# Batch 0 of a fused attention-and-MoE kernel: states first in the load queue, x in four pair loads, attention head pair by head pair, the first S·W as S·W1 − S·W2, and a column of ones for the state-read sums

## The chip, the cores and the metric

The kernel runs on one core of a Trainium2 chip. The metric is the device time of one execution in microseconds (us); of several runs the median is given. An execution is also taken by the hardware profiler; its trace is what the rows below show. The engines are TensorE (PE for matmuls, PEld for loads of its stationary operand), VectorE (DVE), ScalarE (ACT), GpSimd (POOL) and SyncE (SP, which here only issues DMAs). Each engine works off its own list of instructions in the order in which they are written.

## The reference, cut to what matters

```python
B, H, S, Ns, D = 8, 8, 512, 32, 64            # x: B,H,S,D   state: B,H,Ns,D   float32
a     = softmax(scale * x @ state.T)           # over the 32 states
xread = a @ state                              # S rows per batch
a2    = softmax(scale * state @ x.T)           # over the 512 tokens
sread = a2 @ x                                 # Ns rows per batch
t = concat([xread, sread], axis=2)             # then tokens x (H*D = 512), 4352 of them
out = maximum(t @ w1, t @ w2) @ w_out          # d_ff = 1024
```

## The kernel before

maximum(h1, h2) is computed as relu(h1 − h2) + h2. So a batch needs t @ (w1 − w2), its relu times w_out, and t @ (w2 w_out). The kernel builds `wd` = w1 − w2 and `wwo` = w2 w_out on the chip, in bf16. For the S rows of a batch t is a @ state, so the kernel multiplies the states into the weights once per batch: `sw` makes SW = state · [wd | wwo], 1024 + 512 columns, in two halves g of four heads each, with the states laid out in block-diagonal pairs of heads in `sbd` (four pairs k of two heads). `l1` then multiplies the transposed attention weights `AT` by SW and applies relu into `R`; `l2` adds R · w_out (`l2_f`) and AT · SW's last 512 columns (`l2_open`) into one PSUM bank per token block c of 128 tokens (NC = 4), copies it out and stores it. `sread_mm` computes the state reads, the unnormalised e.T @ x, and with eight more matmuls of one column each the sums of e that `sread_norm` divides by; `sread_tr` transposes them, and `moe_sread` sends all batches' state reads through the MoE at the end.

The weights come in four quarters q of 256 columns of d_ff: `load_wq` brings w2, w1 and w_out of a quarter (512 KB each), `w2_cast` and `wo_cast` make bf16, `w_sub` subtracts, `w2_tr` transposes w2, `w_wo` adds up w2 w_out. Batch 0 is worked off quarter by quarter as the weights land, with its four l2 sums open in `ACC` for the whole time (that takes the four banks of the PSUM pool `pa`); batch 1's attention (`states` for batches 1 to 7, `cast_x`, `xt_pe`, `scores`, `norm`, `at_pe`) is put between its quarters. This part, up to batch 1's first l1, is called the ramp below. After it a loop runs over the batches 1 to 7: eight l1 blocks, the scores of the next batch, four l2 blocks with `sw` of the next batch between them. Batches 2 to 7 get x transposed by DMA instead of by TensorE.

The schedule is written by hand: every engine, and SP's queue of loads, follows the order of the calls in the code (`engs` and `eng` arguments choose V, A or P for a copy). SP issues a DMA only when its buffer is free and when an earlier DMA has landed (eight at a time are under way). `idle(n)` issues n matmuls on zeros. A pool's buffer comes free when its last reader is done.

Of the kernel before, what the change touches and what calls it, by code (L numbers as in the profile page):

```python
# [15 lines left out]
def kernel(  # L16
# [59 lines left out]
    sfr = stage.tile([112, 2, 512], F32, name="sfr")  # L76
    sbr = stage.tile([112, 8, 2, D], BF16, name="sbr")
    sread_t = consts.tile([128, 4, B * Ns], BF16, name="sread_t")
# [3 lines left out]

    def load_x(b):
        xf = xio.tile([128, H, NC * D], F32, tag="xf", name="xf")
        xf_t[b] = xf
        for g in range(2):
            nc.sync.dma_start(
                out=xf[:, 4 * g:4 * g + 4, :],
                in_=x[b, 4 * g:4 * g + 4].rearrange("h (p c) d -> p h (c d)", c=NC),
            )  # L90
# [9 lines left out]

    def load_states(t, lo, hi):
        s = state[lo:hi].rearrange("b (k j) (l m) d -> (b k) l j (m d)", j=2, l=4)
        if hi - lo == 1:
            for j in range(2):
                nc.scalar.dma_start(out=t[:, j, :], in_=s[:, :, j, :])
        else:
            for j in range(2):
                nc.sync.dma_start(out=t[:, j, :], in_=s[:, :, j, :])


    def states(sf, sb, lo, hi, ceng, e0, e1, pool=None):
        nb = hi - lo
        copy(ceng, sb.rearrange("p m j d -> p j m d"), sf.rearrange("p j (m d) -> p j m d", m=8))
        p = bank(BF16, pool)
        n = nb * 16
        for m in range(8):
            nc.tensor.transpose(p[:, m * n:(m + 1) * n], sb[:, m].rearrange("p j d -> p (j d)"), ident[0:n, 0:n])
        for j, e in ((0, e0), (1, e1)):
            o = sbd[64 * j:64 * j + 64, lo:hi, :, 32 * j:32 * j + 32].rearrange("p b k (l m) -> p (b k) l m", l=4)
            i = p[64 * j:64 * j + 64, 0:8 * n].rearrange("p (m k l) -> p k l m", m=8, l=4)  # L120
            copy(e, o, i)


# [26 lines left out]
    def scores(b, hh, pool=None):  # L150
        d = st[b]
        if hh == 0:
            d["e"] = at.tile([128, 2, NC, 4, Ns], BF16, tag="e", name="e")
            d["a"] = at.tile([128, 2, NC, 4, Ns], BF16, tag="a", name="a")
            d["es"] = at.tile([128, 2, 2 * NC, 2], F32, tag="es", name="es")
            d["er"] = at.tile([128, 2, 2 * NC, 2], F32, tag="er", name="er")
# [38 lines left out]
    def sread_mm(b, pool=None):  # L195
        d = st[b]
        p = bank(F32, pool)
        d["srp"] = p
        for c in range(NC):
            xv = d["xb"][:, c].rearrange("p (i g d) -> p g i d", g=2, d=D)  # L200
            for g in range(2):
                for ih in range(2):
                    nc.tensor.matmul(p[64 * ih:64 * ih + 64, g * 128:(g + 1) * 128],  # L203
                                     d["e"][:, g, c, 2 * ih:2 * ih + 2].rearrange("p i n -> p (i n)"),
                                     xv[:, g, 2 * ih:2 * ih + 2],
                                     start=(c == 0 and g == 0), stop=(c == NC - 1 and g == 1), skip_group_check=True)
        for g in range(2):
            for c in range(NC):
                nc.tensor.matmul(p[:, 256 + g:257 + g], d["e"][:, g, c].rearrange("p i n -> p (i n)"), ones[:, 0:1],  # L209
                                 start=False, stop=(c == NC - 1), skip_group_check=True)  # L210

    def sread_norm(b):
# [4 lines left out]
        d["sr"] = sr  # L217
        nc.vector.reciprocal(rr, p[:, 256:258])
        for g in range(2):
            nc.vector.tensor_scalar(sr[:, :, g, :], p[:, g * 128:(g + 1) * 128].rearrange("p (i d) -> p i d", i=2),  # L220
                                    scalar1=rr[:, g:g + 1], scalar2=None, op0=ALU.mult)

# [10 lines left out]
    def sw(b, lo, hi, engs=("V", "A"), pool=None):  # L233
# [9 lines left out]
        for g in range(2):  # L243
            copy(engs[g], SW[b][:, g, lo:hi], pg[g][:, 0:n])

    flip = [0]
# [45 lines left out]
    def moe_sread():  # L292
        NT = B * Ns
        r = big.tile([128, NF, NT], BF16, tag="rs", bufs=1, name="rs")
        for f in range(NF):
# [4 lines left out]
            relu(r[:, f, :], p[:, 0:NT])  # L300
        ob = big.tile([128, NT // 128, DM], F32, tag="obs", bufs=1, name="obs")
        for t in range(NT // 128):
# [30 lines left out]

    def w_wo(half, i):
        p = bank()
        for j in range(4):
            f = 4 * half + j
            nc.tensor.matmul(p, w2t[:, f, i, :], wo[:, f, :], start=(j == 0), stop=(j == 3))  # L338
        if half == 0:
            copy("A" if i % 2 else "V", w2acc[:, i, :], p)  # L340
        else:
            nc.vector.tensor_tensor(wwo[:, i, :], p, w2acc[:, i, :], op=ALU.add)

    def idle(n):
        p = bank(F32, pa)
        for j in range(n):
            nc.tensor.matmul(p, wz[:, 0:128], wz, start=True, stop=True)

# [5 lines left out]


    load_states(sf0, 0, 1)
    load_x(0)
    for q in range(3):
        load_wq(q)
    load_states(sfr, 1, B)  # L360
    load_x(1)
# [9 lines left out]


    idle(7)
    states(sf0, sb0, 0, 1, "V", "A", "V", pa)
    cast_x(0, ("V", "V"))
    xt_pe(0, 0, "A", pa)
    xt_pe(0, 1, "V", pa)
    w2_cast(0, "P")
    scores(0, 0)
    w2_tr(0, "A")  # L380
    norm(0, 0, "V")
    scores(0, 1)
# [69 lines left out]
    for b in range(1, B):  # L452
# [61 lines left out]
```

## Time and profile before

| | us |
|---|---|
| median of 3 runs | 171.64 (171.13 to 173.83) |
| the profiled execution, its own time | 172.71 |
| its span, first to last instruction | 170.9 |
| PE busy in the span | 147.9 (87%) |
| DVE, ACT, POOL busy | 89.7, 66.6, 38.0 |

The profiled execution's own time stands 0.6% over the median of the runs. The span is 1.8 us shorter than its own time. Busy shares are averages over a ramp in which PE waits and a loop in which it does not, so they are to be read stretch by stretch.

### The profile page before, as it was taken

Reading aid. Unit: us, or ns where it says so; the run is one execution under the profiler, and the core shown is the slowest. Engines: PE = TensorE matmul, PEld = TensorE weight load, DVE = VectorE, ACT = ScalarE, POOL = GpSimd, SP = SyncE. Lnnn points to the kernel's source line nnn. Section 1 sums busy time; section 2 is a strip of 40 time slices with the busy share of each in tenths; the row PEclk is TensorE's granted clock in tenths of the full one; section 3 lists DMA queues with packets and bytes.
Section 4 is the critical chain, followed back from the end, with each engine's and each line's share of the span. In section 5 each row is a group of like instructions: output and inputs, shape, how many; then the busy total and the mean of one; then the engine's idle time right before and its main releaser. Section 6 shows DMA issues by size and latency. Waiting matters only on the chain.

```text
span 170.9 us, 2878 instructions
## 1 busy us (share of the span) xinstructions
PE 147.9 (87%) x1164; PEld 73.7 (43%) x1183; DVE 89.7 (52%) x163; ACT 66.6 (39%) x127; POOL 38.0 (22%) x41
## 2 busy tenths in 40 slices
PE   7053769959498999999999999999999999999990
PEld 2043534545253344453444445444444544574440
DVE  2158663663667692475458248645815854551110
ACT  3024424365414753382255237316424631730111
POOL 1055361200850031404043040403400040000000
PEclk9999999987999999999999999999999999999999
DMA  5999999910060497598948559685830620501333
GB/s 172 318 373 359 292 324 356 339 47 4 2 119 4 180 125 184 192 271 117 288 157 217 125 183 296 110 266 186 194 61 2 247 52 10 244 6 39 85 123 123
DMA packets 34561, 29.02 MB, mean 170 GB/s; under 512 B 19572, under 2 KB 31860, under 8 KB 33652
## 3 DMA queue, kind: packets, MB, share of 16 engines
q1 hardware_dynamic: 34508, 28.77, 59.3%
q8 instruction: 9, 0.15, 0.3%
q10 hardware_dynamic: 40, 0.07, 0.1%
q14 instruction: 4, 0.03, 0.1%
HBM read 15.20 MB, written 8.91 MB: 141 GB/s over the span
## 4 chain that ended last, share of the span: by engine, by line
PE 80%; DVE 8%; ACT 4%; DMA 3%; issue 2%; ACTq 1%; DVEq 0%
PE acc L274 33%; PE ps L264 16%; PE acc L270 9%; PE ps L241 4%; PE ps L338 4%; DMA sf<-in_state_dram 3%; PE ps L203 2%; PE ps L298 2%; PE ps L162 2%; PE acc L308 2%; DVE xb L60 2%; DVE wd L328 1%; PE ps L209 1%; DVE es L172 1%; PE acc L306 1%
## 5 line engine op out<-in xcount | busy, mean ns | idle before, releaser
L274 PE MATMUL acc<-wo,r 128*128 128x512 bf16 x252 | 60.7, 383 | 0.4 <-ACT xt L58 0.2
L274 PEld LDWEIGHTS <-r 128*128 128x128 bf16 x256 | 25.1, 99 | 30.1 <-issue 1.3
L264 PE MATMUL ps<-aT,sw 128*128 128x512 bf16 x127 | 30.2, 385 | 3.2 <-DVE sw L60 2.8
L255 DVE TENSOR_SCALAR r<-ps 128x512 bf16<-128x512 f32 x32 | 22.1, 692 | 19.6 <-PE ps L264 19.6
L58 ACT CAST sw<-ps 128x512 bf16<-128x512 f32 (+1 forms) x26 | 14.3, 555 | 33.3 <-PE ps L241 23.0
L174 POOL TENSOR_TENSOR a<-e,er 128x512 bf16<-128x512 bf16 x14 | 14.4, 1049 | 56.7 <-DVE er L173 42.6
L253 ACT ACTIVATE r<-ps 128x512 bf16<-128x512 f32 x32 | 19.3, 604 | 9.0 <-PE ps L264 7.7
L60 DVE CAST sw<-ps 128x512 bf16<-128x512 f32 (+1 forms) x26 | 16.5, 643 | 11.1 <-PE ps L241 11.0
L60 DVE COPY ob<-acc 128x512 f32<-128x512 f32 x16 | 10.8, 672 | 21.8 <-PE acc L274 21.6
L58 ACT COPY ob<-acc 128x512 f32<-128x512 f32 x16 | 9.4, 585 | 27.7 <-PE acc L274 26.8
L264 PEld LDWEIGHTS <-sw 128*128 128x128 bf16 x128 | 12.1, 99 | 16.5 <-DVE sw L60 3.1
L62 POOL CAST xb<-xf 128x1024 bf16<-128x1024 f32 x12 | 12.3, 1039 | 23.4 <-DMA xf<-in_x_dram 23.4
L270 PE MATMUL acc<-sw,aT 128*128 128x512 bf16 x52 | 16.2, 381 | 1.0 <-DVE sw L60 0.2
L172 DVE TENSOR_REDUCE es<-e 128x16 f32<-128x512 bf16 x16 | 10.6, 661 | 4.0 <-ACT e L165 3.9
L165 ACT ACTIVATE e<-ps 128x512 bf16<-128x512 f32 x16 | 8.8, 595 | 3.4 <-PE ps L162 2.6
L241 PE MATMUL ps<-wd,sbd 64*32 64x512 bf16 (+1 forms) x144 | 7.2, 369 | 2.2 <-DVE wd L328 1.7
L241 PEld LDWEIGHTS <-sbd 64*32 64x32 bf16 x208 | 3.3, 89 | 11.6 <-issue 11.3
L328 POOL TENSOR_TENSOR wd<-w1f,w2f 128x512 bf16<-128x512 f32 x4 | 5.1, 1267 | 9.6 <-DMA w1f<-in_moe_w_dram 9.6
L338 PE MATMUL ps<-wo,w2t 128*128 128x512 bf16 x31 | 7.0, 379 | 0.1
L270 PEld LDWEIGHTS <-aT 128*128 128x128 bf16 x64 | 4.4, 97 | 4.8 <-issue 3.1
L162 PEld LDWEIGHTS <-xt 128*128 128x128 bf16 x128 | 5.4, 103 | 1.7
L162 PE MATMUL ps<-sbd,xt 128*128 128x64 bf16 x128 | 5.7, 200 | 0.0
(78 smaller groups left out, 119.0 us busy)
## 6 DMA issues: line engine op xcount, KB each, us to landing
xf<-in_x_dram SPq DMA_DIRECT2D x16, 512.0 KB, 4.9
out_dram<-ob SPq DMA_DIRECT2D x7, 1024.0 KB, 5.7
w2f<-in_moe_w_dram SPq DMA_DIRECT2D x4, 512.0 KB, 9.9
w1f<-in_moe_w_dram SPq DMA_DIRECT2D x4, 512.0 KB, 11.1
wof<-in_moe_w_out_dram SPq DMA_DIRECT2D x4, 512.0 KB, 10.6
out_dram<-ob SPq DMA_DIRECT2D x2, 512.0 KB, 2.6
out_dram<-obs SPq DMA_DIRECT2D x8, 64.0 KB, 1.7
sfr<-in_state_dram SPq DMA_DIRECT2D x2, 224.0 KB
```

The lines of the kernel that those rows point to most:

```text
L58: nc.scalar.copy(o, i)
L60: nc.vector.tensor_copy(o, i)
L162: nc.tensor.matmul(pv[:, c, kk], d["xt"][:, c, k, :], sbd[:, b, k, :], start=(c == 0 and kk == 0), stop=(c == NC - 1 and kk == 1))
L172: nc.vector.tensor_reduce(d["es"][:, hh], ev, axis=mybir.AxisListType.X, op=ALU.add)
L174: (nc.gpsimd if eng == "P" else nc.vector).tensor_mul(av, ev, d["er"][:, hh].unsqueeze(3).to_broadcast([128, 2 * NC, 2, Ns]))
L241: nc.tensor.matmul(pg[g][32 * i:32 * i + 32, 0:n], sbd[64 * g:64 * g + 64, b, i, 32 * g:32 * g + 32], rhs, start=True, stop=True)
L253: nc.scalar.activation(out=o, in_=p, func=ACTF.Relu)
L255: nc.vector.tensor_scalar(o, p, scalar1=0.0, scalar2=None, op0=ALU.max)
L264: nc.tensor.matmul(p, SW[b][:, g, f * 128:(f + 1) * 128], AT[b][:, g].rearrange("p c t -> p (c t)"), start=(g == 0), stop=(g == 1))
L270: nc.tensor.matmul(p, AT[b][:, g, c, :], SW[b][:, g, FF:WC], start=(start and g == 0), stop=(stop and g == 1))
L274: nc.tensor.matmul(p, R[b][:, f, c * 128:(c + 1) * 128], wo[:, f, :], start=(start and j == 0), stop=(stop and j == len(fs) - 1))
L338: nc.tensor.matmul(p, w2t[:, f, i, :], wo[:, f, :], start=(j == 0), stop=(j == 3))
```

## The change

Five things are done. First, the states of batch 0 are loaded by one DMA at the head of SP's queue into 128 partitions (before: two DMAs on ACT's queue into 16 partitions); one transpose then gives `sbd` of batch 0 where eight did, and a negated copy `sbdn` is made. Second, x of batch 0 is loaded in four DMAs of one head pair each, and cast (POOL), transposed, scored and normalised pair by pair. Third, the first 256 columns of SW are computed as sbd · w1 + sbdn · w2 from bf16 copies of w1 and w2 (`sw_first`), so that they do not wait for wd. Fourth, for batches 2 to 7 a copy of x in bf16 with a 65th column of ones per head (`xo`) feeds `sread_mm`, and the eight matmuls of one column go; `cast_x1` makes the copy on POOL. Fifth, the order of the ramp is rewritten: `w_sub` goes to one engine per quarter (POOL, V, V, V), `w_wo` is done in three parts of 2, 4 and 2 blocks, fillers (`idle`) stand between the steps of the head, and in the loop all three parts of `sw` stand together behind the second l2.

```diff
-    sf0 = stage.tile([16, 2, 512], F32, name="sf0")
-    sb0 = stage.tile([16, 8, 2, D], BF16, name="sb0")
+    sf0 = stage.tile([128, 2 * D], F32, name="sf0")
+    sb0 = stage.tile([128, 2 * D], BF16, name="sb0")
+    sbdn = stage.tile([128, 4, 2 * Ns], BF16, name="sbdn")
+    w1b = stage.tile([128, 4, FQ], BF16, name="w1b")
...
+    def load_state0():
+        nc.sync.dma_start(out=sf0.rearrange("p (j d) -> p j d", j=2),
+                          in_=state[0].rearrange("(k j) n d -> n k j d", j=2))
+
+    def state0():
+        nc.vector.tensor_copy(sb0, sf0)
+        p = bank(BF16, pa)
+        nc.tensor.transpose(p[:, 0:128], sb0, ident)
+        for j, e in ((0, "A"), (1, "V")):
+            copy(e, sbd[64 * j:64 * j + 64, 0, :, 32 * j:32 * j + 32],
+                 p[64 * j:64 * j + 64, 0:128].rearrange("p (n k) -> p k n", k=4))
+        nc.vector.tensor_scalar(sbdn, sbd[:, 0], scalar1=-1.0, scalar2=None, op0=ALU.mult)
...
+    def cast_x1(b):
+        xo = stage.tile([128, NC, H, 66], BF16, tag="w1f", bufs=3, name="xo")
+        nc.gpsimd.memset(xo[:, :, :, 64:65], 1.0)
+        for g in range(2):
+            nc.gpsimd.tensor_copy(xo[:, :, 4 * g:4 * g + 4, 0:D].rearrange("p c i d -> p i c d"),
+                                  xf_t[b][:, 4 * g:4 * g + 4, :].rearrange("p i (c d) -> p i c d", c=NC))
...
+    def sw_first(engs):
+        SW[0] = big.tile([128, 2, WC], BF16, tag="sw", name="sw")
+        pg = [bank(), bank()]
+        for t, w in ((sbd[:, 0], w1b), (sbdn, w2b[0])):
+            for i in range(4):
+                for g in range(2):
+                    nc.tensor.matmul(pg[g][32 * i:32 * i + 32, 0:FQ], t[64 * g:64 * g + 64, i, 32 * g:32 * g + 32],
+                                     w[64 * g:64 * g + 64, i, :], start=(w is w1b), stop=(w is not w1b))
+        for g in range(2):
+            copy(engs[g], SW[0][:, g, 0:FQ], pg[g][:, 0:FQ])
...
-    load_states(sf0, 0, 1)
-    load_x(0)
+    load_state0()
+    load_x(0, 4)
...
+    idle(3)
+    state0()
+    idle(2)
+    for k in range(4):
+        cast_pair(0, k, "P")
+    xt_pair(0, 0, "A")
...
+    norm_pair(0, 0, "P")
     w2_cast(0, "P")
+    scores_pair(0, 2)
+    idle(2)
+    norm_pair(0, 1, "P")
+    scores_pair(0, 3)
+    copy("P", w1b.rearrange("p i f -> p (i f)"), w1f[0].rearrange("p i f -> p (i f)"))
+    norm_pair(0, 2, "V")
+    norm_pair(0, 3, "V")
...
+    w2_tr(0, "A")
+    sread_mm(0, pa)
+    idle(1)
+    sw_first(("A", "V"))
+    at_pe(0, ("A", "V"))
     wo_cast(0, "P")
...
+    for i in range(4):
+        w_wo((0, 1), i, "A" if i % 2 else "V", first=True)
+    w_sub(1, 0, 4, "V")
+    w_sub(0, 0, 4, "P")
...
         for c in range(NC):
             l2(b, c)
             if n < B:
-                if c < 3:
-                    sw(n, 512 * c, 512 * c + 512)
                 if c == 1:
+                    sw_all(n)
                     sread_mm(n)
```

On SP the head of the queue stood so before; xf is x, sfr the states of batches 1 to 7, and the states of batch 0 were on ACT's queue:

```order
L87 DMA xf<-in_x_dram 128x4x256 x2
L97 DMA w2f<-in_moe_w_dram 128x4x256
L97 DMA w1f<-in_moe_w_dram 128x4x256
L99 DMA wof<-in_moe_w_out_dram 128x2x512
L97 DMA w2f<-in_moe_w_dram 128x4x256
```

It stands so now:

```order
L106 DMA sf_90<-in_state_dram 128x2x64
L90 DMA xf<-in_x_dram 128x2x256 x4
L100 DMA w2f<-in_moe_w_dram 128x4x256
L100 DMA w1f<-in_moe_w_dram 128x4x256
L102 DMA wof<-in_moe_w_out_dram 128x2x512
```

One small DMA is ahead of x, x comes in four parts, and the weights keep their order behind it.

On POOL, from the first instruction that waits for a load, the ramp's work stood so before, up to batch 1's attention weights:

```order
L62 CAST w2b<-w2f 128x1024 [waits DMAHW4_49]
L328 TENSOR_TENSOR wd<-w1f,w2f 128x2x256 [waits DMAHW5_49]
L62 CAST wo<-wof 128x1024 [waits DMAHW6_49]
L328 TENSOR_TENSOR wd<-w1f,w2f 128x2x256 [waits DMAHW7_49,DMAHW0_49]
L62 CAST wo<-wof 128x1024 [waits DMAHW1_49]
L328 TENSOR_TENSOR wd<-w1f,w2f 128x2x256 [waits DMAHW3_49,DMAHW2_49]
L62 CAST wo<-wof 128x1024 [waits DMAHW4_49]
L62 CAST sbr<-sfr 112x2x8x64 [waits DMAHW6_49,DMAHW5_49]
L328 TENSOR_TENSOR wd<-w1f,w2f 128x2x256 [waits DMAHW2_49,DMAHW1_49]
```

It stands so now, where a<-e,er is the softmax product of one head pair:

```order
L62 CAST xb<-xf 128x2x4x64 x4
L194 TENSOR_TENSOR a<-e,er 128x8x32
L62 CAST w2b<-w2f 128x1024
L194 TENSOR_TENSOR a<-e,er 128x8x32
L62 CAST w1b<-w1f 128x1024
L62 CAST wo<-wof 128x1024
L416 TENSOR_TENSOR wd<-w1f,w2f 128x4x256
L62 CAST wo<-wof 128x1024 x2
L62 CAST sbr<-sfr 128x2x8x64
L62 CAST xb<-xf 128x4x4x64
L62 CAST w2b<-w2f 128x1024
```

POOL now casts x of batch 0 and w1 of quarter 0 ahead of the first w_out, makes the whole of wd's quarter 0 later, and no other quarter's.

On DVE, from the subtraction of quarter 2 to the first reduction of batch 1 (es<-e), the ramp stood so before:

```order
L328 TENSOR_TENSOR wd<-w1f,w2f 128x2x256 [waits DMAHW3_49,DMAHW2_49]
L60 COPY w2t<-ps 128x1024 [waits PE_49]
L60 CAST sw<-ps 128x256 [waits PE_49]
L60 COPY sbd<-ps 64x28x32 [waits Activation_49]
L60 CAST xb<-xf 128x4x4x64 [waits DMAHW7_49]
L255 TENSOR_SCALAR r<-ps 128x512 [waits PE_49]
L60 COPY xt<-ps 128x4x256 [waits PE_49]
L328 TENSOR_TENSOR wd<-w1f,w2f 128x2x256 [waits DMAHW2_49,DMAHW1_49]
L172 TENSOR_REDUCE es<-e 128x16 [waits Activation_49]
```

It stands so now:

```order
L416 TENSOR_TENSOR wd<-w1f,w2f 128x4x256 [waits DMAHW4_49,DMAHW3_49]
L60 CAST sw<-ps 128x256 [waits PE_49]
L429 TENSOR_TENSOR w2acc<-ps,w2acc 128x512 [waits DVE_49,PE_49]
L429 TENSOR_TENSOR w2acc<-ps,w2acc 128x512 [waits PE_49,Activation_49]
L429 TENSOR_TENSOR w2acc<-ps,w2acc 128x512 [waits DVE_49,PE_49]
L429 TENSOR_TENSOR w2acc<-ps,w2acc 128x512 [waits PE_49,Activation_49]
L343 TENSOR_SCALAR r<-ps 128x512 [waits PE_49]
L60 COPY sbd<-ps 64x28x32 [waits Activation_49]
L60 COPY xt<-ps 128x4x256 [waits PE_49]
L60 COPY w2t<-ps 128x1024 [waits PE_49]
L416 TENSOR_TENSOR wd<-w1f,w2f 128x4x256 [waits DMAHW3_49,DMAHW2_49]
L233 TENSOR_REDUCE es<-e 128x16 [waits Activation_49]
```

DVE's subtractions are twice as wide, its cast of x of batch 1 is gone (POOL has it), and four additions of the middle part of w2 w_out stand ahead of batch 1.

## Rows read from the trace of the kernel before

**Rows 1.** Busy time by engine in two stretches, ramp and loop.

```profile
core 0: us, PE busy (x) PEld busy (x) DVE busy (x) ACT busy (x) POOL busy (x), PEclk, DMA share, GB/s
20.80:57.20 36.40, 29.60 (x246) 15.49 (x248) 22.10 (x39) 15.35 (x27) 10.60 (x10) 0.95 0.49 144
57.20:170.90 113.70, 108.33 (x829) 51.56 (x841) 56.71 (x108) 44.66 (x92) 20.64 (x20) 1.00 0.57 153
```

**Rows 2.** Chain that ended last, first 21 us (start us, us, what).

```profile
2.03 5.64 DMA sf<-in_state_dram
...
9.53 2.15 DVE xb L60 x2
```

**Rows 3.** DMA issues, 0 to 1.2 and 1.2 to 1.75; last: us to landing.

```profile
xf<-in_x_dram SPq DMA_DIRECT2D x1, 512.0 KB, 3.5
...
xf<-in_x_dram SPq DMA_DIRECT2D x1, 512.0 KB, 4.8
```

**Rows 4.** Timeline of POOL: start us, us, what, idle before and why.

```profile
10.02 1.10 POOL L62 CAST w2b<-w2f 128x1024 bf16<-128x1024 f32 x1 [8.72 <-DMA w2f<-in_moe_w_dram]
11.52 1.27 POOL L328 TENSOR_TENSOR wd<-w1f,w2f 128x512 bf16<-128x512 f32 x1 [0.40 <-DMA w1f<-in_moe_w_dram]
```

**Rows 5.** Timeline of DVE.

```profile
13.85 0.69 DVE L172 TENSOR_REDUCE es<-e 128x16 f32<-128x512 bf16 x1 [0.36 <-ACT e L165]
...
16.34 0.25 DVE L173 RECIPROCAL er<-es 128x16 f32<-128x16 f32 x1
16.63 1.07 DVE L174 TENSOR_TENSOR a<-e,er 128x512 bf16<-128x512 bf16 x1
17.62 1.52 DVE L328 TENSOR_TENSOR wd<-w1f,w2f 128x512 bf16<-128x512 f32 x1
...
24.01 0.68 DVE L328 TENSOR_TENSOR wd<-w1f,w2f 128x512 bf16<-128x512 f32 x1
```

**Rows 6.** Timeline of ACT.

```profile
35.05 1.04 ACT L58 CAST xb<-xf 128x1024 bf16<-128x1024 f32 x1
```

**Rows 7.** Timeline of PE.

```profile
10.29 1.03 PE L146 MATMUL acc<-ident,xb 128*128 128x128 bf16 x8 [1.40 <-DVE xb L60]
...
20.77 0.59 PE L264 MATMUL ps<-aT,sw 128*128 128x512 bf16 x1
21.58 1.06 PE L264 MATMUL ps<-aT,sw 128*128 128x512 bf16 x2 [0.22 <-issue]
...
24.98 1.90 PE L274 MATMUL acc<-wo,r 128*128 128x512 bf16 x8
...
37.06 1.79 PE L146 MATMUL ps<-ident,xb 128*128 128x128 bf16 x16 [1.42 <-DVE xb L60]
...
45.14 1.04 PE L264 MATMUL ps<-aT,sw 128*128 128x512 bf16 x4 [2.42 <-DVE sw L60]
...
57.47 3.18 PE L264 MATMUL ps<-aT,sw 128*128 128x512 bf16 x14 [0.17 <-ACT sw L58]
```

**Rows 8.** Busy time and granted clock, one stretch; columns as in rows 1.

```profile
37.50:40.50 3.00, 2.78 (x17) 1.90 (x17) 1.51 (x3) 1.96 (x2) 0.00 (x0) 0.50 0.00 0
```

**Rows 9.** Chain that ended last, over one batch of the loop.

```profile
71.97 3.45 PE ps L264 x16
...
78.05 0.34 PE ps L241 x8
78.39 0.54 PE acc L270 x2
...
81.56 0.28 PE ps L209 x8
...
86.74 0.21 PE ps L264
```

**Rows 10.** Groups of instructions in the loop, POOL's two.

```profile
L174 POOL TENSOR_TENSOR a<-e,er 128x512 bf16<-128x512 bf16 x12 | 12.3, 1049 | 45.2 <-DVE er L173 31.1 <-ACT e L165 14.1
...
L62 POOL CAST xb<-xf 128x1024 bf16<-128x1024 f32 x8 | 8.3, 1038 | 23.4 <-DMA xf<-in_x_dram 23.4
```

More of the change, by code (lines that the diff above doesn't have):

```diff
@@ new lines, in state0, with load_states @@
+    def state0():
[6 more added lines that the diff above has]
+        nc.vector.tensor_scalar(sbdn, sbd[:, 0], scalar1=-1.0, scalar2=None, op0=ALU.mult)
+    def load_states():
+        s = state.rearrange("b (k j) (l m) d -> (b k) l j (m d)", j=2, l=4)
+        for j in range(2):
+            nc.sync.dma_start(out=sfr[:, j, :], in_=s[:, :, j, :])
@@ new lines, in xt_pair, with att_tiles @@
+    def xt_pair(b, k, eng):
+        d = st[b]
+        if k == 0:
+            d["xt"] = at.tile([128, NC, 4, 128], BF16, tag="xt", name="xt")
+        p = bank(BF16)
+        for c in range(NC):
+            nc.tensor.transpose(p[:, c * 128:(c + 1) * 128], d["xb"][:, c, k * 128:k * 128 + 128], ident)
+        copy(eng, d["xt"][:, :, k, :], p[:, 0:512].rearrange("p (c t) -> p c t", c=NC))
+    def att_tiles(b):
+        d = st[b]
+        d["e"] = at.tile([128, 2, NC, 4, Ns], BF16, tag="e", name="e")
+        d["a"] = at.tile([128, 2, NC, 4, Ns], BF16, tag="a", name="a")
+        d["es"] = at.tile([128, 2, 2 * NC, 2], F32, tag="es", name="es")
+        d["er"] = at.tile([128, 2, 2 * NC, 2], F32, tag="er", name="er")
@@ new lines, in scores_pair @@
+    def scores_pair(b, k):
+        d = st[b]
+        if k == 0:
+            att_tiles(b)
+        p = bank(F32, pa)
+        for c in range(NC):
+            nc.tensor.matmul(p[:, c * 64:c * 64 + 64], d["xt"][:, c, k, :], sbd[:, b, k, :],
+                             start=(c == 0), stop=(c == NC - 1))
+        nc.scalar.activation(out=d["e"][:, :, :, k, :].rearrange("p g c n -> p c g n"),
+                             in_=p[:, 0:256].rearrange("p (c g n) -> p c g n", c=NC, g=2), func=ACTF.Exp, scale=scale)
@@ L206, in sread_mm @@
                                      start=(c == 0 and g == 0), stop=(c == NC - 1 and g == 1), skip_group_check=True)
[L207 to L210, printed above, removed]
+        if "xo" not in d:
+            for g in range(2):
+                for c in range(NC):
+                    nc.tensor.matmul(p[:, 256 + g:257 + g], d["e"][:, g, c].rearrange("p i n -> p (i n)"), ones[:, 0:1],
+                                     start=False, stop=(c == NC - 1), skip_group_check=True)
     def sread_norm(b):
@@ L332, in wo_cast, with w_wo, idle @@
         copy(eng, wo[:, 2 * q:2 * q + 2, :], wof[q])
-    def w_wo(half, i):
+    def w_wo(fs, i, eng, first=False, last=False):
         p = bank()
[L336 to L340, printed above, removed]
-        else:
-            nc.vector.tensor_tensor(wwo[:, i, :], p, w2acc[:, i, :], op=ALU.add)
-    def idle(n):
-        p = bank(F32, pa)
+        for j, f in enumerate(fs):
+            nc.tensor.matmul(p, w2t[:, f, i, :], wo[:, f, :], start=(j == 0), stop=(j == len(fs) - 1))
+        if first:
+            copy(eng, w2acc[:, i, :], p)
+        else:
+            nc.vector.tensor_tensor(wwo[:, i, :] if last else w2acc[:, i, :], p, w2acc[:, i, :], op=ALU.add)
+    idle_p = [None]
+    def idle(n, cols=512):
+        if idle_p[0] is None:
+            idle_p[0] = bank(F32, pa)
         for j in range(n):
-            nc.tensor.matmul(p, wz[:, 0:128], wz, start=True, stop=True)
+            nc.tensor.matmul(idle_p[0][:, 0:cols], wz[:, 0:128], wz[:, 0:cols], start=True, stop=True)
     def l2_part(q, first):
@@ L446 @@
         l2_out(0, c, ACC[c], "A" if c % 2 else "V")
+        if c == 1:
+            sw(1, 0, 512)
+        if c == 2:
+            sw(1, 512, 1024)
     sw(1, FF, WC)
@@ L464 @@
             at_dma(n)
+            if b + 2 < B:
+                cast_x1(b + 2)
             if b + 3 < B:
```

166 lines of the change are left out of this document (87 added, 79 removed).

## The prediction

> **What bounds the kernel now.** I read the busy time by stretch first. In the loop (57.2 to 170.9) PE is busy 108.3 of 113.7 us [rows 1], and the chain over one batch consists of PE alone: one batch is 86.74 − 71.97 = 14.77 us of back-to-back matmuls [rows 9]. There only fewer or denser matmuls help. In the 36.4 us of the ramp PE is busy 29.6 [rows 1], though a part of that is slow running. And before 20.77, the first l1 [rows 7], the chain is no PE work at all: it waits 5.64 us for the states of batch 0, then DVE casts x for 2.15 us, then come softmax, the subtraction of wd at 17.62 and the first SW [rows 2, 5]. So three terms carry the sum: the head (0 to 20.77), the ramp (20.77 to 57.2, batch 1's l1: its last 14 of 16 matmuls start at 57.47 at 0.216 each) [rows 7], and the loop.
>
> PE's level has to be read from the spacing. The profile grants a clock of 1.00 up to 34 us, yet two 512-column matmuls at 21.58 take 1.06 us, 0.43 apart, and eight at 24.98 take 1.90, 0.216 apart [rows 7]: the first is 1.2 GHz, the second 2.4. All matmul rows before about 24 us run at the lower one, after stretches in which PE often stood idle. It falls again, to a granted 0.50 from 37.5 to 40.5 [rows 8], after a hole of 1.42 us that follows a thin stretch [rows 7].
>
> **The head.** *States.* One 64 KB DMA replaces the two on ACT's queue. The first half of x, issued at 0.73, lands 3.5 us later, the second, issued 0.5 later, after 4.8: at 4.2 and 6.0, so 512 KB take 1.8 us and some 1.7 pass before [rows 3]. The states land between 2.6 (that start and their bytes) and 4.2 (as late as a half of x), instead of at 7.67 [rows 2]. They then lie ahead of x and cost the chain nothing but the half microsecond of issue by which x is later.
> One rule speaks against this load: it reads runs of 256 bytes. The Trainium skill ("DMA: Bandwidth & Descriptors", Specifications) asks for at least 512 bytes a piece for line rate. By that the load would take about twice its byte time, an estimate of 0.4 us instead of 0.2, and the sum below would be 9.6 instead of 9.8; no row here shows a load of such runs alone.
>
> *x.* Pairs of 256 KB land at about 3.9, 4.7, 5.6 and 6.5. POOL casts 512 elements where 1024 cost 1.04 [rows 10]: 0.52 each, the last done at 7.05 (before: DVE at 11.68 [rows 2]). Pair 3 then needs four transposes at 0.13 (0.5, [rows 7]), a copy, scores and exp (about 1.1 with their hand-overs, and two fillers before its scores, 0.9), a reduction and a reciprocal (0.36 and 0.25: half, and the whole, of [rows 5]) and the product. Attention of batch 0 is done by about 11.4; the second product of before ended at 17.70 [rows 5].
>
> *The weights take over.* w2 of quarter 0 lands at 10.0 and w1 at 11.5 [rows 4], and nothing moves these much: the same bytes are ahead. POOL: w2 cast 10.0 to 11.1, the second pair's product 0.55, w1 cast 1.04, so to 12.7. The subtraction of 1.52 on DVE [rows 5] is off the path, which is what the two-part product buys; its eight more matmuls cost about 0.4. PE meanwhile has w2's transposes from 11.1 (1.04 at 1.2 GHz, half at 2.4), the state reads (1.3 or 0.9) and a filler. So the first SW starts at 12.8 or 13.9, takes 0.6 or 0.84, its copy and the transposes and copies of a another 1.0, two fillers stand before l1: first l1 at 14.6 if PE is up, 16.7 if not. I take 15.7, **5.1 us earlier**. Bounds: 6.3 earlier (all at 2.4), 3 earlier (1.2 GHz and loads a microsecond late).
>
> **The ramp.** Its PE work is the same but for the order: 88 matmuls of 512 columns for l1, w2 w_out and l2 at 0.216 (19.0), SW 2.3 (0.34 a part [rows 9]), 60 transposes 4.0 (half of the 0.13 at 1.2 GHz), batch 1's scores and state reads some 1.3: 26.6 us at 2.4 GHz. Of the 36.4 us [rows 1] that leaves 9.8: about 3.1 from the lower level (3.7 us at the start with PE three quarters busy, 3.4 us in the middle, half of each) and 6.7 of waits, the longest 2.42 for SW behind DVE's list and 1.42 for x of batch 1 [rows 7]. I followed the new lists with the old durations from a first l1 at 14.6. Waits that go: DVE's subtractions of quarters 1 and 2 stand ahead of need, and w2 w_out needs eight matmuls instead of sixteen behind quarter 3. Waits that come: w2's casts on ACT stand ahead of a relu (about 1.2 in all); x of batch 1's second half is cast on ACT (1.04, [rows 6]) only behind the copy of the states, with TensorE's transposes behind it (1.4); the subtraction of quarter 3, 1.36 on DVE (twice 0.68, [rows 5]), stands behind two copies, with SW's last quarter behind it (1.5); the copy of that SW stands behind two reductions and reciprocals (1.1); the last of four additions into wwo holds l2 (0.8). With small ones 6.4: as much as before. Batch 1's l1 comes 33.0 us after the first. What is gained is the level, if it holds: 3.4; if it falls once more, 1.7. I take **3.0 us**. Bounds: 4.5 (a wait of 1.1 less than I see), nothing.
> The loads allow that: quarter 2 and batch 1's x were needed before they were late; the last transposed x (batch 2, cast on POOL by about 41.5) is wanted at 51, and the DMA that transposes it has ten microseconds.
>
> **POOL against DVE.** This speaks against the change: POOL works nearly without a break from 4 to 17 us, and DVE's products and subtractions lie beside it. The rows show the price: the subtraction of 0.68 alone took 1.52 at 17.62, the product 1.07 at 16.63, while POOL was at work [rows 5]. DVE has five such operations on or near the new path (two products, three subtractions); at 0.4 to 0.85 each that is some 3 us if all wait. POOL's list has gaps behind its loads, and my steps hold 0.5 of it; the rest is a rival. The Trainium skill ("GPSIMD Engine Reference", 8. Key points) has it as a rule that GpSimd shares its SBUF interfaces with VectorE and contends with instructions of two SBUF inputs. By that rule all five would wait, and the sum would be 7.3 instead of 9.8; the two rows agree with it.
>
> **The loop.** Per batch the eight one-column matmuls go, 0.28 [rows 9]; 65 columns per head for 64 cost nothing visible. An l2 behind an SW part takes 0.54 for its first two matmuls where 0.43 (two at 0.216) would do [rows 9]; two of these places go, 0.22. Against that, the state reads now take a bank that DVE must first copy out: its copy of 0.69 ends some 0.2 after the last SW matmul. Net 0.28, six times: **1.7 us**. Bounds: 3.0 and 0. POOL's two more casts per batch (2.1 us on top of 4.1, from [rows 10]: 1.04 and 1.05 twice each) stay below 14.5, behind the products, so no one waits for them.
>
> **Sum.** 5.1 + 3.0 + 1.7 = 9.8 us. The profiled execution took 172.71, so 162.9 by it; on the median of the runs, 171.64, it is **161.8 us**. The bounds of the three terms added, 13.8 and 3, are not met together; 158 to 165 is this case's own range.
>
> **The rivals.**
> *Given back in the ramp.* The head is faster, but the ramp's waits grow by what it came earlier: the casts on ACT and the shared port lie on PE's path. For it: I count as many waits as before, each by a list written by hand. Against: PE's work is there, and the loads are ahead of it. The ramp then loses 0.6, the loop gives 0.9 and the head 5.1, together 5.4: 166.2.
> *POOL and DVE in turns.* All five operations wait, on the path, 3 us where I hold 0.5: 2.5 less, 164.3. For it: both rows in which they met. Against: the one subtraction that PE waits for directly, quarter 3's, stands where POOL waits for it in turn.
> *The head isn't shorter.* Four DMAs on one queue share the engines and land together near 7, and the weights at 10.0 and 11.5 hold the rest; with PE at 1.2 GHz the first l1 comes at 18, 2.8 earlier, the ramp loses 1.4 by running low for longer, the loop gives 1.7: 3.1 in all, 168.5. For it: w2 lands 4 us after x today, so loads do overlap.
> *Slower.* PE stays at 1.2 GHz through the ramp: waits of 1 to 1.5 us, now shorter but more of them, keep it from rising. The 26.6 us of work become 53; with the waits half hidden batch 1's l1 starts near 70 instead of 57.2, less 1.7: near 183. It outweighs the gain once PE runs low for some 20 us of busy time in the ramp (half of that is the 9.8). For it: it ran low for 24 us at the start and fell after one hole. Against: the fillers and the denser head, and 2.4 GHz held across the 2.42 us hole at 42.7 [rows 7].
>
> **The numbers.** Forecast 0.58, given back 0.16, in turns 0.12, no shorter head 0.09, slower 0.05. The range reaches to the first two rivals and a little beyond, 157.5 to 167. What a measurement can tell from no change is about 2%, so faster is below 168.2: the forecast and the first two rivals, 0.86 less their tails, 0.84; within 2%, 0.11; slower, 0.05.
>
> **What would show it.** Right: the states landing before 4.3 and POOL's fourth cast ending near 7; first l1 at 14.6 to 16.7; spacing 0.216 from then on; batch 1's l1 at 47.5 to 51; a loop batch of 14.3 to 14.5. Wrong: a granted clock of 0.50 for over 4 us in the ramp, DVE's subtractions at over 2 us, or a hole in front of the state reads of over 0.4 us per batch.

## The result, and the profile after

The kernel after takes 164.49 us in the median of 4 runs (163.53 to 165.27); the kernel before, on the same chip, 172.74 (171.13 to 175.56). The ratio is 0.9595, 95% interval 0.9478 to 0.9712: faster by 4.0%. This ratio and those below leave out runs of over 1.5% above the fastest of their kernel, so they aren't the quotients of the medians. The time lies within the predicted range, 2.7 us above the forecast of 161.8. The profiled execution took 165.27, its span 163.6.

The busy time by stretch, cut at the first l1 and at batch 1's first l1 matmul, columns as in [rows 1]:

```profile
core 0: us, PE busy (x) PEld busy (x) DVE busy (x) ACT busy (x) POOL busy (x), PEclk, DMA share, GB/s
0.00:16.50 16.50, 12.39 (x102) 6.52 (x103) 7.72 (x20) 6.33 (x12) 9.37 (x16) 1.00 0.85 275
16.50:50.30 33.80, 29.29 (x245) 13.97 (x244) 23.09 (x41) 16.60 (x28) 14.40 (x15) 0.95 0.68 211
50.30:163.60 113.30, 106.31 (x797) 51.17 (x795) 56.97 (x108) 43.88 (x93) 30.83 (x35) 1.00 0.55 154
```

The prediction cut the kernel before at 57.2, but two l1 matmuls of batch 1 stand ahead of the fourteen in [rows 7]. They are these, so batch 1's l1 begins at 56.71 there:

```profile
56.71 0.59 PE L264 MATMUL ps<-aT,sw 128*128 128x512 bf16 x2
```

The head went from 20.77 to 16.51, the ramp behind it from 35.94 to 33.83, and the loop to the end of the span from 114.19 to 113.26: −4.26, −2.11 and −0.93, together the 7.3 us by which the span is shorter. Forecast were −5.1, −3.0 and −1.7; cut at 57.2 as there, 0.49 of the loop's gain would count for the ramp.

**The head.** The chain that ended last, with start and duration:

```profile
0.73 0.74 SPq L106
...
2.67 0.47 SPq L90
3.14 0.04 issue
3.18 4.60 DMA xf<-in_x_dram
7.78 0.05 issue
7.84 0.63 POOL xb L62
8.46 0.05 issue
8.51 0.62 PE ps L165 x4
...
9.94 0.21 DVE er L193
...
10.30 0.42 POOL a L194
10.72 0.15 issue
10.86 1.05 POOL w2b L62
11.91 0.05 issue
11.96 1.04 PE ps L411 x8
...
14.74 0.56 PE ps L324 x11
```

The wait for the states [rows 2] is gone; the last pair of x stands in its place, issued at 3.18 behind 2.25 us of issues on SP and landed at 7.78. From there the chain goes through the attention of that pair to DVE's reciprocal, from it to POOL's first product, and only then to the cast of w2. A load of weights isn't in it. The loads themselves, KB each and (median) us to landing, as in [rows 3], with the first load of w2, issued at 3.70:

```profile
xf<-in_x_dram SPq DMA_DIRECT2D x4, 256.0 KB, 3.5
w2f<-in_moe_w_dram SPq DMA_DIRECT2D x1, 512.0 KB, 6.5
...
sf<-in_state_dram SPq DMA_DIRECT2D x1, 64.0 KB, 2.4
```

So w2 of quarter 0 landed at 10.2, 0.7 before POOL's cast of it began.

**The ramp.** The timeline of PE, where it waited, and the first and the slow l1:

```profile
16.51 1.02 PE L352 MATMUL ps<-aT,sw 128*128 128x512 bf16 x4
...
22.32 1.04 PE L352 MATMUL ps<-aT,sw 128*128 128x512 bf16 x4 [0.33 <-DVE sw L60]
...
32.91 0.62 PE L210 MATMUL ps<-ident,xb 128*128 128x128 bf16 x8 [1.49 <-ACT xb L58]
...
37.62 0.30 PE L312 MATMUL ps<-wd,sbd 64*32 64x256 bf16 x8 [1.45 <-DVE wd L416]
...
39.62 1.88 PE L352 MATMUL ps<-aT,sw 128*128 128x512 bf16 x4 [0.84 <-DVE sw L60]
...
46.97 1.02 PE L358 MATMUL acc<-sw,aT 128*128 128x512 bf16 x4 [0.28 <-DVE sw L60]
```

The holes of [rows 7] (1.42, 2.42) have become 1.49, 1.45 and 0.84. Four matmuls of l1 take 1.02 at 16.51 and 1.88 at 39.62: behind the two last holes the clock is at its lower level once more, as in [rows 8]. Busy time and granted clock there:

```profile
39.70:43.00 3.30, 3.30 (x9) 1.10 (x9) 1.43 (x5) 0.60 (x1) 3.30 (x5) 0.50 0.00 0
```

**The loop.** The chain over one batch, to be read against [rows 9]:

```profile
65.25 3.45 PE ps L352 x16
...
74.05 0.60 ACT sw L58
74.69 0.67 PE ps L268 x16
75.36 0.54 PE acc L358 x2
...
79.89 3.45 PE ps L352 x16
```

One batch takes 14.64 us, 0.13 less than before. The ones are gone, but ACT now stands in a chain that was PE alone: the state reads (L268) wait for its copy of an SW part. The list of PE's waits says how often and how long (sum in us, times, the longest):

```profile
PE ps L268 <- ACT sw L58: 2.6, 6, 0.4
```

### The profile page after: what moved, and what is told of

It is laid out like the page before. It is cut to its first block, busy times and chain, and to the rows that moved or that the text cites. A ratio compares the mean times of both kernels' runs of the same rounds, so it can differ in the third digit from the quotient of the medians.

```text
span 163.6 us, 2847 instructions
## 1 busy us (share of the span) xinstructions
PE 148.0 (90%) x1142; PEld 71.7 (44%) x1142; DVE 87.8 (54%) x167; ACT 66.8 (41%) x131; POOL 54.6 (33%) x65
## 4 chain that ended last, share of the span: by engine, by line
PE 71%; issue 12%; ACT 6%; DVE 3%; DMA 3%; SPq 1%; POOL 1%; POOLq 0%
PE acc L362 25%; PE ps L352 17%; PE acc L358 8%; PE ps L425 5%; DMA xf<-in_x_dram 3%; PE ps L268 2%; ACT ob L58 2%; PE ps L386 2%; PE acc L396 2%; ACT sw L58 2%; PE ps L223 2%; PE ps L411 2%; PE ps L312 1%; PE acc L394 1%; SPq L90 1%
## 5 line engine op out<-in xcount | busy, mean ns | idle before, releaser
L62 POOL CAST xb<-xf 128x1024 bf16<-128x1024 f32 (+1 forms) x17 | 16.4, 974 | 21.3 <-DMA xf<-in_x_dram 21.2
L60 DVE CAST sw<-ps 128x512 bf16<-128x512 f32 (+1 forms) x20 | 12.0, 630 | 14.4 <-PE ps L312 12.9
L358 PE MATMUL acc<-sw,aT 128*128 128x512 bf16 x64 | 19.0, 380 | 0.3 <-DVE sw L60 0.3
L58 ACT CAST sw<-ps 128x512 bf16<-128x512 f32 (+1 forms) x20 | 10.3, 551 | 8.6 <-PE ps L312 7.3
L149 POOL CAST xo<-xf 128x1024 bf16<-128x1024 f32 x12 | 12.2, 1044 | 0.0
L233 DVE TENSOR_REDUCE es<-e 128x16 f32<-128x512 bf16 x14 | 9.2, 656 | 1.5 <-ACT e L226 1.5
L437 PE MATMUL acc<-wz 128*128 128x512 bf16 x13 | 6.4, 586 | 1.2 <-DVE ones L457 1.2
L268 PEld LDWEIGHTS <-e 128*64 128x64 bf16 x128 | 4.3, 116 | 5.9 <-ACT sw L58 5.5
L312 PE MATMUL ps<-wd,sbd 64*32 64x512 bf16 (+1 forms) x136 | 5.5, 364 | 1.4 <-DVE wd L416 1.4
L268 PE MATMUL ps<-xo,e 128*64 128x130 bf16 x96 | 4.0, 224 | 2.6 <-ACT sw L58 2.6
```

The costliest lines, as they stand in the source:

```text
L58: nc.scalar.copy(o, i)
L60: nc.vector.tensor_copy(o, i)
L62: nc.gpsimd.tensor_copy(o, i)
L149: nc.gpsimd.tensor_copy(xo[:, :, 4 * g:4 * g + 4, 0:D].rearrange("p c i d -> p i c d"), xf_t[b][:, 4 * g:4 * g + 4, :].rearrange("p i (c d ...
L268: nc.tensor.matmul(p[64 * ih:64 * ih + 64, g * 2 * m:(g + 1) * 2 * m], d["e"][:, g, c, 2 * ih:2 * ih + 2].rearrange("p i n -> p (i n)"), x ...
L358: nc.tensor.matmul(p, AT[b][:, g, c, :], SW[b][:, g, FF:WC], start=(start and g == 0), stop=(stop and g == 1))
```

## The experiments

Ratios are to the kernel before on the same chip (0.9595 for the changed kernel), diffs to the changed kernel. My theory after the result: the head and the ramp went as forecast, smaller by what holds POOL's cast of w2 and by one fall of the clock; the loop's gain is eaten by the state reads' bank. The rivals: wider state reads, pieces and fillers that cost what they bring, POOL and DVE in turns.

**The state reads get a bank of the other pool.**

```diff
-                    sread_mm(n)
+                    sread_mm(n, pa)
```

> Only the loop differs: the state reads take a bank of the pool pa instead of ps. Theory (the loop's gain went into the 0.43 us hole in front of the state reads, where they wait for a copy of SW to free a bank): the hole goes, a loop batch falls from 14.64 to about 14.2, the loop from 113.3 to 110.8, the time by 2.4 us to about 162. Rival A (the hole is the time that ACT is late with the copies, so it moves to the next l2, which waits for a bank or for ACT in turn): a batch stays at 14.6, the time at 164.5. Rival B (the casts of xo on POOL or its 66-column rows slow the loop): a batch stays at 14.6 with the state reads at 0.66 and no hole to be seen elsewhere.

Measured: 160.83 us, ratio 0.9338 (0.9160 to 0.9515). The profiled execution, 162.77, was the longest of the four, so only its loop is read:

```profile
73.53 0.56 PE ps L312 x16
74.08 0.22 PE acc L312 x8
74.30 0.59 PE acc L268 x15
74.89 0.32 PE acc L358
```

The hole is gone, and a batch takes 14.13 (65.29 to 79.42). Six times 0.51 is 3.1; the loop to the end of the span is 110.26, 3.0 shorter. The bank accounts for the whole of the hole.

**No column of ones (the eight matmuls of one column back).**

```diff
-    cast_x1(2)
...
-            if b + 2 < B:
-                cast_x1(b + 2)
```

> No xo: no casts of it on POOL, and the eight one-column matmuls are back for batches 2 to 7; SW stays in one piece. Theory: the hole is a matter of banks and stays at about 0.43, the eight matmuls add 0.28 to 0.37, a loop batch takes 14.9 to 15.0, the time rises by about 2 us to 166.5. Rival (xo's cost on POOL or in the reads eats what the eight matmuls give): a batch stays at 14.6 or falls, the time stays at 164.5 or falls.

Measured: 165.62 us, ratio 0.9612 (0.9436 to 0.9788); a batch takes 14.82 (65.08 to 79.90), and the hole is still 0.43. So the column is worth 0.18 per batch, some 1.1 us in six. The time, 1.1 above the changed kernel's, can't be told from it. What ate the loop's gain isn't the column, which brings less than the 0.28 expected.

**The subtraction of quarter 3 on POOL instead of DVE.**

```diff
+    w_sub(3, 0, 4, "P")
...
-    w_sub(3, 0, 4, "V")
```

> wd of quarter 3 is subtracted on POOL, which is idle there from 28.9 to 38.6, instead of on DVE. Theory (the ramp's two holes of 1.45 and 0.84 us at 36 and 39 come from DVE's list, and the fall of PE's clock at 39.7 from the holes): quarter 3 of wd is ready before DVE is done with w2t, the first hole goes or shrinks to under 0.3, the second stays near 0.8, the clock stays at 1.00 through 39 to 43, batch 1's l1 comes 1.5 to 3 us earlier, at 47.3 to 48.8. Rival (POOL and DVE take turns in SBUF, so DVE's reductions become as much later): batch 1's l1 within 0.7 of 50.3, the holes move.

Measured: 161.78 us (161.46 to 162.08), ratio 0.9425 (0.9354 to 0.9496). Waits of PE at the same places:

```profile
31.39 0.62 PE L210 MATMUL ps<-ident,xb 128*128 128x128 bf16 x8 [1.49 <-ACT xb L58]
...
37.23 1.04 PE L352 MATMUL ps<-aT,sw 128*128 128x512 bf16 x3 [0.71 <-DVE sw L60]
```

Its ramp, from the first l1 to batch 1's:

```profile
14.99:46.67 31.68, 28.08 (x240) 13.75 (x244) 21.78 (x40) 16.53 (x28) 18.01 (x16) 1.00 0.77 241
```

The first l1 stands at 14.99, since PE was at the higher level early in this execution (see the last section). Behind it the 1.45 is gone, the 0.84 became 0.71, and the clock stayed up (1.00). The ramp is 2.1 shorter: PE idles 3.60 us for 4.51, since some small holes came, and is busy 28.08 for 29.29, about what the slow stretch had cost.

**No fillers in the head** (all seven calls for matmuls on zeros left out).

```diff
-    idle(3)
...
-    idle(2)
...
-    idle(1)
```

> All 13 fillers are left out. Theory (the fillers bring PE to 2.4 GHz earlier, and what they cost in the head is hidden behind POOL's casts): the head's matmuls run at 0.43 a 512-column matmul until 18 or later, first l1 at 16.5 to 17.5, batch 1's l1 1 to 2 us later than 50.3, time 165.5 to 166.5. Rival (the fillers stand in the way): first l1 at 15.5 to 16.0 and batch 1's l1 earlier than 50.3.

Measured: 165.37 us, ratio 0.9560 (0.9391 to 0.9728): no difference that can be told. The first l1 came at 15.42, 1.1 earlier, but its first three matmuls took 1.44, so at the lower level; the l1 of the next quarter stands at 22.20 against 22.32. What the fillers take in the head, the later rise gives back. I had expected the first l1 at 16.5 at the earliest, and a longer time. Batch 1's l1 came at 48.95 for 50.34; of this 1.3 lie behind 39.5, where the clock fell in the changed kernel and didn't fall here.

**The states as before** (two DMAs on ACT's queue, eight transposes; all else as after).

```diff
+        s = state[0:1].rearrange("b (k j) (l m) d -> (b k) l j (m d)", j=2, l=4)
+        for j in range(2):
+            nc.scalar.dma_start(out=sf0[:, j, :], in_=s[:, :, j, :])
...
+        for m in range(8):
+            nc.tensor.transpose(p[:, m * 16:(m + 1) * 16], sb0[:, m].rearrange("p j d -> p (j d)"), ident[0:16, 0:16])
```

> The states of batch 0 come as before: two DMAs on ACT's queue into 16 partitions, eight transposes. Theory (the early states are what lets pair after pair be scored while x lands): the states land at 7 to 8 instead of 3.1, the first scores start at about 9.3 instead of 6.5, the last at 12.5 to 13, first l1 1.5 to 2.5 us later, the time about 2 us longer. Rival (w1 of quarter 0 and POOL's casts hold the first SW at 14.7 anyway): first l1 within 0.6 of 16.5.

Measured: 165.94 us, ratio 0.9545 (0.9456 to 0.9633). The cast of the states starts at 5.79 instead of 3.15, the first scores at 8.98 instead of 6.50, the transposes of w2 at 13.33 instead of 11.96. Yet its first l1 stands at 16.48, beside 16.51, because in this execution PE was at the higher level from 11.5 on. Against the kernels whose PE was up before w2's transposes too (14.99 above, 14.96 in the next) it is 1.5 late. So the states' load is worth some 1.4 to 1.5 us of the head here, and it was on the path; the ratio alone can't show it.

**x of batch 0 in two halves instead of four pairs.**

```diff
-    load_x(0, 4)
+    load_x(0, 2)
```

> x of batch 0 comes in two DMAs of four heads, as before, and is still cast and scored pair by pair. Theory (the pieces matter little, since the last piece lands as before and only one more cast of 0.62 stands behind it): first l1 0.2 to 0.7 later. Rival A (the pair loads carry the head): 1.5 us or more later. Rival B (two issues less, so the weights land a microsecond earlier): first l1 earlier by 0.3 to 1.

Measured: 163.18 us, ratio 0.9413 (0.9337 to 0.9489); first l1 at 14.96. POOL's casts start at 5.31 and 7.05 where the four pairs' start between 4.55 and 7.84: the pieces bring the first pair sooner and the last one later, and the path needs the last. With PE up as early, four pairs had the first l1 at 14.99 (quarter 3 on POOL): the pieces bring nothing that shows. The shorter time than the changed kernel's isn't the halves' doing either: in this execution PE was up early and the clock didn't fall in the ramp.

**The first SW from wd again** (a half of its subtraction on each of POOL and DVE).

```diff
-    copy("P", w1b.rearrange("p i f -> p (i f)"), w1f[0].rearrange("p i f -> p (i f)"))
+    w_sub(0, 2, 4, "P")
...
+    w_sub(0, 0, 2, "V")
...
-    sw_first(("A", "V"))
+    sw(0, 0, FQ, ("A", "V"))
...
-    w_sub(0, 0, 4, "P")
```

> The first 256 columns of SW are computed from wd again, its quarter 0 subtracted half on POOL, half on DVE, in place of the cast of w1. Theory (by the trace after, DVE is free at 13.9 and POOL at 12.7, so wd would be there at about 15): SW starts at 15.0 to 15.4 instead of 14.7, first l1 0.3 to 0.8 later, and POOL gets 2.35 us less to do later. Rival (the prediction's: the subtraction of 1.5 us comes back on the path in full): first l1 1.3 us or more later.

Measured: 165.97 us (165.47 to 166.33), ratio 0.9570 (0.9507 to 0.9634). DVE and PE in turn:

```profile
12.74 1.39 DVE L194 TENSOR_TENSOR a<-e,er 128x256 bf16<-128x256 bf16 x1
14.05 1.52 DVE L416 TENSOR_TENSOR wd<-w1f,w2f 128x512 bf16<-128x512 f32 x1
```

```profile
15.63 0.42 PE L312 MATMUL ps<-wd,sbd 64*32 64x256 bf16 x8 [2.23 <-DVE wd L416]
...
17.65 1.45 PE L352 MATMUL ps<-aT,sw 128*128 128x512 bf16 x4
```

The 1.52 of [rows 5] is back to the digit, while POOL casts w_out (13.80 to 15.03); the product ahead of it took 1.39 beside POOL's half of the subtraction (12.58 to 13.85). SW starts 1.0 later than in the changed kernel (14.67), 2.1 later than where PE was up (13.57), and PE falls to the lower level in the hole. By these places the product in two parts is worth more than I expected of this run; the ratio doesn't show it, since here the clock didn't fall in the ramp.

**The bank and quarter 3 on POOL together** (the two edits above).

```diff
+    w_sub(3, 0, 4, "P")
...
-                    sread_mm(n)
+                    sread_mm(n, pa)
```

> The state reads' bank from pa and quarter 3's subtraction on POOL together. Theory (the two holes have nothing to do with each other): a loop batch of 14.14, batch 1's l1 31.5 to 32 us after the first l1, time 158.5 to 159.5, under both alone. Rival: the ramp or the loop gives back, 160.5 or more.

Measured: 160.24 us, ratio 0.9207 (0.9109 to 0.9305). By places they add: a batch of 14.13, batch 1's l1 (48.85) 31.97 behind the first (16.88). The time is 0.7 above the range expected.

**POOL casts w2 ahead of the first product.**

```diff
-    norm_pair(0, 0, "P")
     w2_cast(0, "P")
+    norm_pair(0, 0, "P")
```

> POOL casts w2 of quarter 0 ahead of the first pair's softmax product instead of behind it. Theory (after the change the weights are there in time, and w2's cast stands at 10.86 only because POOL's list has a product before it that waits for DVE): the cast starts at 8.5 to 9.8, its transposes a microsecond or more before 11.96, first l1 by 0.3 to 1 earlier where PE's level is the same. Rival (the prediction's step: w2 lands at 10.0 whatever is changed): the cast starts at 9.9 to 10.1 with a wait for the DMA, and the first l1 moves by less than 0.3.

Measured: 163.70 us, ratio 0.9500 (0.9427 to 0.9574). POOL:

```profile
9.16 1.04 POOL L62 CAST w2b<-w2f 128x1024 bf16<-128x1024 f32 x1 [0.91 <-DMA w2f<-in_moe_w_dram]
10.17 1.20 POOL L194 TENSOR_TENSOR a<-e,er 128x256 bf16<-128x256 bf16 x2
11.31 1.23 POOL L62 CAST w1b<-w1f 128x1024 bf16<-128x1024 f32 x1
```

Now the load is what the cast waits for, and it lands at 9.1. SW starts at 12.59, the first l1 at 14.01, with PE up. In the changed kernel the cast stood 1.7 later, behind a product that waited for DVE; 1.1 of these are the load's, which landed at 10.2 there.

**Both casts ahead of it.**

```diff
-    norm_pair(0, 0, "P")
     w2_cast(0, "P")
+    copy("P", w1b.rearrange("p i f -> p (i f)"), w1f[0].rearrange("p i f -> p (i f)"))
+    norm_pair(0, 0, "P")
...
-    copy("P", w1b.rearrange("p i f -> p (i f)"), w1f[0].rearrange("p i f -> p (i f)"))
```

> POOL casts w2 and w1 of quarter 0 ahead of the first two softmax products. Theory as for the run above, and w1 landing by about 10.5: SW starts before 13, the products are done by 13.5, first l1 at 14.5 to 16. Rival (w1 lands at 11.5, as the prediction had it): its cast starts at 11.5 with a wait for the DMA, the products come after 12.6, and the first l1 is no earlier than 15 at 2.4 GHz or 16.5 at 1.2.

Measured: 163.13 us, ratio 0.9447 (0.9376 to 0.9519). SW at 12.93, the first l1 at 14.76: the cast of w1 starts at 10.90, only 0.4 sooner, and the products come later, so that PE waits 0.35 for the last. No further gain.

**Three of them together: bank, quarter 3 on POOL, w2 first.**

```diff
-    norm_pair(0, 0, "P")
     w2_cast(0, "P")
+    norm_pair(0, 0, "P")
...
+    w_sub(3, 0, 4, "P")
...
+                    sread_mm(n, pa)
```

> The state reads' own bank, quarter 3's subtraction on POOL, and POOL's cast of w2 ahead of product 0, together. If the three lie on different stretches of the path, they add: the first l1 at 14.0 to 15.0 (16.88 with the first two alone), batch 1's l1 some 32 us behind it, so at 46 to 47 (48.85), a loop batch of 14.14, and a time near 158.5. Rival: the ramp gives the earlier head back, because its loads are no earlier: batch 1's l1 stays at 48 or later, and the time at 160.2, that of the first two.

Measured: 158.53 us (158.23 to 159.69), ratio 0.9101 (0.9031 to 0.9171). w2 landed at 9.9 this time, and the first l1 stands at 14.79; batch 1's l1 at 46.48, a batch is 14.13 (60.94 to 75.07). The bank and quarter 3 keep their places behind the first l1. The earlier cast is worth only 0.2 here: in the run with quarter 3 alone, with product 0 ahead of the cast, w2 landed at 9.7, PE was up as early, and the first l1 stood at 14.99. The rest of what this head has on the 16.88 of the two alone is the clock's.

**The same three with x in two halves.**

```diff
-    load_x(0, 4)
+    load_x(0, 2)
```

> The same three, and x of batch 0 loaded in two halves instead of four pairs. If the pieces bring the head nothing, the first l1 stays within 0.3 us of the other's at the same clock and the time within 1 us. If the four pieces do hasten the head once POOL's cast of w2 doesn't stand behind product 0, this one has its first scores some 0.5 us later and its first l1 0.5 to 1 us later, and is slower by as much.

Measured: 158.64 us (157.84 to 159.44), ratio 0.9089 (0.9027 to 0.9150); first l1 at 14.08, 0.7 earlier, which I hadn't expected: w2 landed at 9.0 for 9.9. The same time on the same chip: the four pieces bring nothing here either.

## Why the prediction came out as it did

**The head went as forecast but for the last pair of x and POOL's list; the ramp's gain came from another place than forecast; the term of the loop was mis-sized by a wait.** All three terms came out smaller than forecast.

*The head* (5.1, measured 4.26). The states landed at 3.1, within the bounds, and the run with the old load shows that this was needed. x came later than forecast: the issues of the states and of three pairs take SP until 3.1, and the last pair landed at 7.78, not 6.5, so POOL's fourth cast ended at 8.46, not 7.05. w2 of quarter 0 landed at 10.2 where the forecast had 10.0. The step that failed is that POOL casts it as it lands, at 10.0: the cast waited at the entry ahead, for product 0 and DVE's list behind the last pair of x, and began at 10.86. What the swap of the two entries brings depends on the load, which landed at 9.0 to 10.2 in the runs. With PE up early, the first l1 came at 14.08 for 14.96 where w2 landed at 9.0 (both with x in halves), and at 14.79 for 14.99 where it landed at 9.9 and 9.7: 0.9 and 0.2. The 1.5 from 16.51 to 14.99 are the clock's. The two clock cases, 14.6 with PE up and 16.7 without, were both met: with the same head the first l1 stood at 14.99 in one kernel and at 16.42 to 17.01 in four others. That 16.51 is so near 16.7 is in part luck: SW started at 14.67 where that case had 13.9, and PE rose at about 15.7, so the steps behind it took 1.84 for 2.8.

*The ramp* (3.0, measured 2.11). The listed waits came nearly one by one: x of batch 1 on ACT 1.49 for 1.4, quarter 3's subtraction 1.45 for 1.5, the copy of its SW 0.84 for 1.1; the last additions into wwo cost 0.28 for 0.8, and ACT's casts ahead of a relu show no hole. In all PE idled 4.5 us for the 6.4 forecast. Its work was more than 26.6: 29.29 busy, less half of the 3.3 at the lower level, is 27.6. And the clock did fall once, which the forecast had between its two cases. The step that failed is "What is gained is the level": the forecast left the waits as long as before, yet PE's idle time fell from 6.8 [rows 1] to 4.5 (to within some 0.4, since five matmul records are missing from the ramp before). Its busy time stayed, 29.6 with 0.5 of batch 1's l1 in it and now 29.29, though it ran at the lower level for 3.3 us where it had been 6.2: what the level gave, some 1.2, went into the longer work. So the net gain is one of waits, and that the sum came as near as it did is luck. Which of the reordered calls took the waits away isn't shown: no run takes back w_wo in three parts, or the places of the subtractions of quarters 1 and 2. The run with quarter 3 on POOL shows that this wait was on the path: 0.9 us of idling and 1.2 of slow running went with it. Of the nine kernels with both holes, one profiled execution of each, the clock fell behind them in five and stayed up in four; of the four without the first hole it fell in none. So the 1.2 can't be put down to the wait for certain.

*The loop* (1.7, measured 0.93, of which six batches of 0.13 give 0.8). Here the step failed that the state reads' bank is free "some 0.2 after the last SW matmul". The pool has four banks, the first two parts of SW take all of them, and DVE and ACT share the copies; ACT's starts at 74.05 behind a copy of ob and ends at 74.65, and PE starts at 74.69. The bank cost 0.51 per batch. Without it the loop is 110.26 long, 3.9 shorter than before, so the gross gain was also undersized: 0.64 a batch where the forecast had 0.28 and 0.22. The ones give 0.18 of it, and the three SW parts in a row take 0.78 where three apart took 1.02 [rows 9], which wasn't in the forecast; the 0.22 left is the forecast's term for l2 behind an SW part. The prediction had named a hole of over 0.4 there as what would prove it wrong, and so it did, for that term.

*The rivals.* Given back: the ramp didn't lose what the head won. In turns: beside POOL, DVE's two products took 0.96 and 1.14, where half of [rows 5]'s 1.07, itself taken beside POOL, is 0.54, and half of the 0.69 that the same product took at 14.86 in the kernel before, with POOL idle, is 0.35. One of its three subtractions took 1.50 where the others took 1.21 and 1.22. That is 1.3 to 1.7 us in all, but none of it was on the path in this execution: the products are done at 13.92, before their transposes at 15.23, and SW at 14.67 stood behind PE's own list, with POOL's cast of w1 done at 13.64 (where PE was up, SW waited for that cast, 0.26). Where the subtraction is put back on the path, its 1.52 stands in it. The sum of this rival, 7.3, is by chance the one measured between the spans: the shortfall was elsewhere. The rule on the shared interfaces of the Trainium skill ("GPSIMD Engine Reference", 8. Key points) agrees with these rows in kind. A shorter head and no lasting fall of the clock rule out the other two.

## What to carry to other kernels

When matmul groups that each take banks are put together, count the banks of the pool and look at the copy that frees the next one: a producer right behind them waits for the copying engines, and a bank of another pool, where one is free, cost nothing here. When a load comes earlier, follow the list of the engine that uses it: the entry ahead of it becomes the wait, here a product ahead of a cast, and a swap of two lines brought 0.2 to 0.9 us, the more the earlier the load. When a term comes out near its forecast, compare idle and busy time with the reasons given for it: the ramp's gain lay in the waits and not in the clock. Splitting a load brought nothing here, where the path needed its last piece.

## What the runs showed of the hardware

The clock didn't follow the instructions alone. The same list of the head ran at the higher level from about 9.6 us in one execution and from 15.5 to 17.0 in four others, while the profile's column grants 1.00 in all. It reads 1.00 there because the trace has no record of the clock before the rise: its first record starts at 9.58 in the one and at 15.77 in the changed kernel (23.54 in the kernel before), where the spacing of the matmuls changes. So the level of a head is read from the spacing. Scores of the last pair, first the changed kernel, then quarter 3 on POOL:

```profile
9.98 0.42 PE L181 MATMUL acc<-sbd,xt 128*128 128x64 bf16 x4
```

```profile
9.76 0.28 PE L181 MATMUL acc<-sbd,xt 128*128 128x64 bf16 x4
```

Nor did its fall. In the changed kernel and in the one without fillers PE stood idle at the same places (1.45 and 0.84) for the same time; the stretches behind it, first the changed kernel's:

```profile
38.00:40.00 2.00, 1.16 (x25) 0.72 (x22) 1.49 (x5) 0.37 (x1) 1.40 (x2) 0.92 0.00 0
40.00:42.00 2.00, 2.00 (x6) 0.76 (x5) 0.46 (x1) 0.60 (x1) 2.00 (x3) 0.50 0.00 0
```

```profile
38.00:40.00 2.00, 1.10 (x24) 0.74 (x20) 1.37 (x5) 0.28 (x1) 1.52 (x2) 1.00 0.00 0
40.00:42.00 2.00, 1.91 (x8) 0.63 (x7) 1.39 (x5) 0.60 (x1) 2.00 (x3) 1.00 0.00 0
```

One fell to 0.50, the other stayed at 1.00. What decides it stays open; a late rise was worth some 1.5 us in these kernels and a fall some 1.3, as much as the smaller edits, so these are to be told apart by places in the trace and not by times alone. Loads scatter too: w2 of quarter 0, issued at 3.7 behind the same five DMAs, landed between 9.1 and 10.2 in ten executions. An issue by SP isn't free either: 0.74 us for the states' DMA, 0.46 to 0.58 for each pair of x, and the last piece of a split load pays for all of them.
